# Fewer warm-up matmuls, two clamps moved to VectorE, and a residual added through the identity, with new instruction orders on all engines

## The chip, the core and the metric

The program runs on one core of one Trainium2 chip. TensorE multiplies, VectorE, ScalarE and GpSimd work on elements, and SyncE issues nearly all DMAs. The metric is the device time of one execution in microseconds; below 1% of change counts, so times stand to a hundredth.

## The reference

The input x is 2048 tokens of 448 features in bf16. A linear attention block is followed by a gated feed-forward block, each behind a layer norm and with a residual:

```python
h  = x + A_ref(layernorm(x), wqkv, wo)          # 16 heads of 28
h2 = h + B_ref(layernorm(h), w_gate, w_up, w_down)
# A: phi(t) = where(t > 0, t + 1, exp(t)) + 1e-6; pq, pk = phi(q), phi(k)
#    kv = pk^T v, z = sum(pk); o = (pq kv) / (pq z + 1e-6); o @ wo
# B: (gelu(n @ w_gate) * (n @ w_up)) @ w_down, 448 -> 1792 -> 448
```

## The kernel before, in words

The 2048 tokens are 16 tiles of 128. Every piece of work is a task with a name and an engine. Tasks know the buffers that they read and write, from which the waits on semaphores follow; in which order an engine issues its tasks is written out by hand in `ORDERS`, one string for TensorE, ScalarE, VectorE, GpSimd and SyncE each (L14 to L62). An engine takes its string strictly from left to right: a task that waits holds up everything behind it.

- **Start.** `warm1` and `warm0` (L454) are matmuls on ones whose results nobody reads; they run while the first tiles of x land. For each tile t, `bnst`/`bnag` (L462, L463) take mean and variance, `ln`/`rstd` (ScalarE) make 1/sigma, and `norm` writes xn. Tiles 0 to 3 are normalised on VectorE (L486) and transposed by TensorE (`tr`, L495), with `ev` (ScalarE, L523) copying the result to xnT. Tiles 4 to 15 are normalised on GpSimd (L487); `dup` (ScalarE, L525) repeats 64 columns, and SyncE issues one transposing DMA each (`xT4` to `xT15`, L526). SyncE has them in order of their tiles, and only behind `xT15` the loads of wo (`dwo`, four DMAs) and of the gate and up weights (`dwg`, `dwu`, 14 DMAs of 224 KB).
- **K and V.** `k`t and `v`t (L430, the helper through which most matmuls go) project a tile in pairs of 64-row matmuls, one on each half of the array. `ek` (exp, ScalarE L565), `cl` (clamp, GpSimd L566) and `ph` (VectorE L568) make phi(k); `evv` (L570) copies v; `acc`t`a`, `acc`t`b` add the tile to kv. The halves of the array change places between `a` and `b`, and a task with the other assignment waits for the earlier one. `eq`, `cq`, `pq` do for q what `ek`, `cl`, `ph` do for k. `kz1`, `kz2` (L642, L643) copy kv out with a mask.
- **Attention out.** `nd`t is pq times kv; `rd`, `om` (L654, L655) divide. Tiles 0 and 1 go by TensorE: `tro` (transpose, L681), `evo` (ScalarE), `wo` (three matmuls of 128 rows at L688, one of 64 at L689), then on VectorE `hr` (L660: PSUM plus x gives h), `hbnst`, `hbnag`, `normh`, `wrap` (L695: repeat 64 columns), and TensorE's `trh` (7 transposes, L702). From tile 2 on tiles go in pairs: `oT` (transposing DMA of o, L729, issued by SyncE behind the weight loads), `wo2a` and `wo2b` (both tiles), `hr`, the norm on GpSimd, `hT` (transposing DMA). The load of w_down, `dwd`, stands behind `oT3`.
- **Feed-forward.** `gu`n is gate and up for one slice of the 1792 columns, `ge` the gelu (ScalarE L830), `hm` the product (VectorE L832), `down` the last matmul, `out` the residual, `dout` the store. `gu` alternates between two pairs of PSUM banks, so a `gu` waits for the `hm` of the one before the last. `tbl2` loads ScalarE's table for gelu after the last exp.

Of the kernel before, what the change touches and what calls it, by code (L numbers as in the profile page):

```python
# [7 lines left out]
ALU = mybir.AluOpType  # L8
# [222 lines left out]
def bass_sequential_preLN__linear_attn_block__glu_gated_geglu__prompt_kernel(  # L231
# [5 lines left out]
    NG, GW = 4, 112  # L237
    GP = GW + 1
    NJ = FF // 128
    EPS_LN = 1e-5  # L240
    EPS = 1e-6
    HN_R = 4
    HR = 8
    O_R = 4
    QCH = 512
    NQC = S // QCH
    N_PE_TR = 4
    STAT_GROUPS = [[0], [1], [2], [3]] + [[t, t + 1] for t in range(4, T, 2)]
    EV_DVE = cfg.get("ev_dve", ())
    N_DVE_NORM = cfg.get("n_dve_norm", 4)  # L250
    N_PE_A2 = 2
    B1_CHUNKS = [2, 2, 4, 4, 4]
    WARM = 38
    WARM2 = 8
    N_END = 4
    Q_LATE = cfg.get("q_late", 5)
    SPLIT = cfg.get("split", (3, 4, 5, 6, 7))

    G = _Graph()
    es = ExitStack()  # L260
    with es:
# [45 lines left out]
        h_sb = x_sb  # L307
# [35 lines left out]
        def bank(*b):  # L343
            return [b_ps[x] for x in b]
# [568 lines left out]
```

## Time and profile before

| | us |
|---|---|
| three timed runs | 196.19, 196.21, 196.62 (median 196.21) |
| the profiled execution's own time | 196.7 |
| its span, first to last instruction | 194.9 |
| TensorE busy / VectorE / ScalarE / GpSimd | 190.3 / 116.3 / 78.2 / 42.0 |

In the profile PE is TensorE's matmuls, PEld its weight loads, DVE VectorE, ACT ScalarE, POOL GpSimd, SP SyncE; a q behind a name (SPq) is the engine's issue of a DMA. A row of the timeline gives start, length, engine, line, operation, written tile and read tiles, the shape, how many instructions are merged (x), and in brackets the engine's idle time before it with what ended it. Starts count from the first instruction of the span. Starts of single tasks named below are those of such rows.

### The profile page before, as it was taken

Reading aid. Unit: us, or ns where it says so; the run is one execution under the profiler, and the core shown is the slowest. Engines: PE = TensorE matmul, PEld = TensorE weight load, DVE = VectorE, ACT = ScalarE, POOL = GpSimd, SP = SyncE. Lnnn points to the kernel's source line nnn. Section 1 sums busy time; section 2 is a strip of 40 time slices with the busy share of each in tenths; the row PEclk is TensorE's granted clock in tenths of the full one; section 3 lists DMA queues with packets and bytes.
Section 4 is the critical chain, followed back from the end, with each engine's and each line's share of the span. In section 5 each row is a group of like instructions: output and inputs, shape, how many; then the busy total and the mean of one; then the engine's idle time right before and its main releaser. Section 6 shows DMA issues by size and latency. Waiting matters only on the chain.

```text
span 194.9 us, 5336 instructions
## 1 busy us (share of the span) xinstructions
PE 190.3 (98%) x2192; PEld 137.9 (71%) x2192; DVE 116.3 (60%) x301; ACT 78.2 (40%) x205; POOL 42.0 (22%) x90
## 2 busy tenths in 40 slices
PE   7999999999999999999999999999999999999994
PEld 7556658754588977976675577877778779899554
DVE  2989735368998946843967745756735443431512
ACT  3689866669784212220442441233232442411100
POOL 3099974300050310500500500500500000000000
PEclk9999999999999999999999999999999999999999
DMA  6944558999836052152062250172040000010111
GB/s 191 377 116 97 81 110 185 247 248 205 260 103 110 15 101 50 50 105 62 10 129 46 46 106 2 30 117 51 5 94 28 23 0 0 3 47 3 47 47 47
DMA packets 37256, 17.53 MB, mean 90 GB/s; under 512 B 28272, under 2 KB 36336, under 8 KB 37232
## 3 DMA queue, kind: packets, MB, share of 16 engines
q1 hardware_dynamic: 36352, 16.45, 36.8%
q10 hardware_dynamic: 880, 0.75, 1.2%
q8 instruction: 17, 0.28, 0.6%
q14 instruction: 7, 0.06, 0.1%
HBM read 8.72 MB, written 1.84 MB: 54 GB/s over the span
## 4 chain that ended last, share of the span: by engine, by line
PE 96%; issue 1%; ACT 1%; DVE 1%; POOL 0%; DVEq 0%; ACTq 0%; POOLq 0%
PE ps L430 87%; PE ps L780 6%; PE ps L454 2%; DVE x_sb L660 1%; PE ps L495 1%; ACT xn L617 1%; PE ps L681 0%; ACT xnT L523 0%; PE ps L672 0%; DVE x_sb L756 0%; POOL ones_bf L395 0%; POOL eps_t L398 0%; ACT pqT L616 0%; DVEq L196 0%; ACTq L196 0%
## 5 line engine op out<-in xcount | busy, mean ns | idle before, releaser
L430 PE MATMUL ps<-hnT,wgu_sb 64*128 64x512 bf16 (+1 forms) x980 | 90.4, 333 | 0.0
L430 PEld LDWEIGHTS ps<-hnT,wgu_sb 64*128 64x128 bf16 x980 | 64.5, 94 | 18.6 <-DVE hh L832 1.7
L830 ACT ACTIVATE gl<-ps 128x256 bf16<-128x256 f32 x112 | 36.9, 381 | 89.3 <-PE ps L430 88.2
L832 DVE TENSOR_TENSOR hh<-ps,gl 128x256 bf16<-128x256 f32 x112 | 42.5, 415 | 35.7 <-ACT gl L830 31.5
L430 PE MATMUL ps<-wd_sb,hh 64*128 64x448 bf16 x336 | 34.4, 349 | 0.0
L430 PEld LDWEIGHTS ps<-wd_sb,hh 64*128 64x128 bf16 x336 | 25.6, 94 | 6.2 <-DVE x_sb L756 0.2
L430 PE MATMUL ps<-wkv_sb,xnT 64*128 64x448 bf16 x192 | 22.4, 350 | 0.4 <-ACT xnT L523 0.4
L462 DVE BATCH_NORM_STATS2 st<-x_sb 128x6 f32<-128x448 bf16 x32 | 18.7, 611 | 2.6 <-DMA x_sb<-in_A_x_dram 2.6
L756 DVE TENSOR_TENSOR x_sb<-ps,x_sb 128x448 bf16<-128x448 f32 (+1 forms) x17 | 9.9, 591 | 16.6 <-PE ps L430 9.8
L474 POOL TENSOR_SCALAR ln<-mv 128x2 f32<-128x2 f32 x7 | 1.6, 223 | 75.0 <-DVE mv L463 74.9
L568 DVE SCALAR_TENSOR_TENSOR pk<-ps,tm 128x448 bf16<-128x448 f32 x16 | 9.8, 620 | 9.6 <-POOL tm L566 7.1
L430 PE MATMUL ps<-xnT,wq_sb 64*128 64x512 bf16 x112 | 14.9, 377 | 0.2 <-ACT xn L617 0.2
L430 PEld LDWEIGHTS ps<-wkv_sb,xnT 64*128 64x128 bf16 x192 | 10.1, 94 | 6.3 <-issue 0.8
L430 PE MATMUL ps<-wo_sb,oT 64*128 64x448 bf16 x98 | 12.1, 350 | 0.1
L660 DVE TENSOR_TENSOR x_sb<-ps,x_sb 128x448 bf16<-128x448 f32 x16 | 9.4, 618 | 4.6 <-PE ps L430 4.4
L780 PE MATMUL ps<-wd_sb,hh 128*128 128x448 bf16 (+1 forms) x70 | 10.8, 315 | 0.0
L566 POOL TENSOR_SCALAR tm<-e 128x448 bf16<-128x448 bf16 x16 | 8.9, 559 | 6.4 <-ACT e L565 5.5
L487 POOL TENSOR_SCALAR hn<-x_sb,nm,rs 128x448 bf16<-128x448 bf16 x14 | 10.0, 720 | 0.8 <-POOL rs L476 0.2
L565 ACT ACTIVATE e<-ps 128x448 bf16<-128x448 f32 x16 | 8.5, 541 | 3.5 <-PE ps L430 2.2
L780 PEld LDWEIGHTS ps<-wd_sb,hh 128*128 128x128 bf16 x70 | 6.7, 98 | 4.3 <-issue 0.4
L655 DVE TENSOR_TENSOR o_sb<-ps,rd 128x448 bf16<-128x448 f32 x16 | 9.4, 612 | 0.1
L570 ACT ACTIVATE v<-ps 128x448 bf16<-128x448 f32 x16 | 8.4, 542 | 2.1 <-PE ps L430 2.1
(69 smaller groups left out, 140.4 us busy)
## 6 DMA issues: line engine op xcount, KB each, us to landing
out_dram<-x_sb SPq DMA_DIRECT2D x15, 112.0 KB, 1.7
wgu_sb<-in_B_w_gate_dram SPq DMA_DIRECT2D x7, 224.0 KB, 6.1
wgu_sb<-in_B_w_up_dram SPq DMA_DIRECT2D x7, 224.0 KB, 6.4
wd_sb<-in_B_w_down_dram SPq DMA_DIRECT2D x1, 1568.0 KB, 8.3
x_sb<-in_A_x_dram SPq DMA_DIRECT2D x2, 448.0 KB, 5.3
wkv_sb<-in_A_wqkv_dram ACTq DMA_DIRECT2D x2, 336.0 KB, 3.7
x_sb<-in_A_x_dram SPq DMA_DIRECT2D x3, 224.0 KB, 4.2
wo_sb<-in_A_wo_dram SPq DMA_DIRECT2D x2, 336.0 KB, 4.4
```

What stands on the lines that cost most here:

```text
L430: ins = e.matmul(o_, l_, r_, start=s_, stop=p_, **kw)
L462: op("dve", lambda e: e.bn_stats(st[:, t, :], src_ap), [b_src], [b_st[t]], "%sbnst%d" % ("" if mv is mv1 else "h", t), 0.53, key, after=after)
L487: return lambda e: e.tensor_scalar(dst, src[:, t, :], nm[:, t:t + 1], rs[:, t:t + 1], ALU.add, ALU.mult)
L565: act_exp(lambda e: e.activation(e1[:, ie, :], oK, AF.Exp), bank(bk), [b_e1[ie]], "ek%d" % t, _c_act(D), kk)
L566: op("pool", lambda e: e.tensor_scalar(tm1[:, ie, :], e1[:, ie, :], 1.0 + EPS, 0.0, ALU.min, ALU.max), [b_e1[ie]], [b_tm1[ie]], "cl%d" % t ...
L568: op("dve", lambda e: e.scalar_tensor_tensor(pk[:, i, :, 0:GW], psK3, EPS, tm1[:, ie, :].rearrange("p (g e) -> p g e", g=NG), ALU.max, ALU ...
L655: op("dve", lambda e: e.tensor_tensor(o_sb[:, so, oc:oc + D].rearrange("p (a e) -> p a e", e=28), nd3[:, :, 0:28], rd[:, i, :].unsqueeze(2 ...
L660: op("dve", lambda e: e.tensor_tensor(h_sb[:, u, :], ps[:, b, 0:D], x_sb[:, u, :], ALU.add), bank(b) + [b_x[u]], [b_h[u]], "hr%d" % u, 0.5 ...
L756: op("dve", lambda e: e.tensor_tensor(x_sb[:, t, c0:c1], ps[:, bk, c0:c1], h_sb[:, t, c0:c1], ALU.add), bank(bk) + [b_h[t]], [bo], "out%d% ...
L780: ins = e.matmul(ps[:, bk, c0:c1], hh[:, j, hsl(t)], wd_sb[:, j, c0:c1], start=(j == 0), stop=(j == NJ - 1))
L830: G.add("act", lambda e, gi=gi, cs_=cs_, psG=psG: e.activation(gl[:, gi, cs_], psG[:, cs_], AF.Gelu_apprx_tanh), r=bank(BK_G[i]), w=[b_glh ...
L832: op("dve", lambda e, dst=dst, srcU=srcU, srcL=srcL: e.tensor_tensor(dst, srcU, srcL, ALU.mult), bank(BK_U[i]) + [b_glh], [b_ar[j_][t % HR ...
```

## The change

Four edits of code, and all five strings of `ORDERS` written anew.

```diff
+    CL_DVE = cfg.get("cl_dve", (14, 15))
-    WARM = 38
+    WARM = 33
...
-            op("pool", lambda e: e.tensor_scalar(tm1[:, ie, :], e1[:, ie, :], 1.0 + EPS, 0.0, ALU.min, ALU.max),
-               [b_e1[ie]], [b_tm1[ie]], "cl%d" % t, 0.53, kk)
+            op("dve" if t in CL_DVE else "pool", lambda e: e.tensor_scalar(tm1[:, ie, :], e1[:, ie, :], 1.0 + EPS, 0.0, ALU.min, ALU.max),
+               [b_e1[ie]], [b_tm1[ie]], "cl%d" % t, _c_dve(D, 4.0) if t in CL_DVE else 0.53, kk)
...
             def fnwo(e):
                 for g in range(3):
                     e.matmul(ps[:, bh, 0:D], oT[:, so, g, :], wo_sb[:, g, :], start=(g == 0), stop=False)
+                e.matmul(ps[:, bh, 0:D], ident[:], x_sb[:, t, :], start=False, stop=False)
                 return e.matmul(ps[:, bh, 0:D], oT[0:64, so, 3, :], wo_sb[0:64, 3, :], start=False, stop=True)
...
-            res_h(t, bh, ka)
+            op("dve", lambda e: e.tensor_copy(h_sb[:, t, :], ps[:, bh, 0:D]), bank(bh), [b_h[t]], "hr%d" % t, _c_dve(D), ka)
+            ln_stats(t, ps[:, bh, 0:D], b_ps[bh], st2, mv2, b_st2, b_mv2, ka)
...
-            def ftrh(e):
+            def ftrh(e, W):
                 ins = None
-                for k in (0, 1, 2, 4, 5, 6, 3):
+                for n, k in enumerate((0, 1, 2, 4, 5, 6, 3)):
+                    if n in (0, 6):
+                        W(n)
```

`warm0` has 33 matmuls for 38. `cl14` and `cl15` go from GpSimd to VectorE. For tiles 0 and 1, `wo` has a fifth matmul that adds x by the identity, so PSUM holds h itself: `hr` is a copy, and `hbnst` reads PSUM and no longer waits for `hr`. `trh` waits for `normh` at its first transpose and for `wrap` only at its seventh. `pkones` (VectorE's fill of pk) moves ahead of the first statistics.

The order of GpSimd in the K and V stage, of which one line reads (names between `cl4` and `cl8`):

```diff
- cl4 norm10 norm11 cl5 norm13 norm12 cl6 negm14 cq3 cq2 cl7 norm14 opad2 norm15 cl8
+ cl4 norm13 cl5 norm10 negm14 norm11 cl6 opad2 cq3 cq2 cl7 norm12 norm14 cl8 norm15
```

On GpSimd before, in the program's rows from `cl5` to `norm15` (L566 with tm<-e is a `cl`, L626 a `cq`, L487 with xn a `norm`, L481 a `negm`, L404 is `opad2`):

```order
L566 TENSOR_SCALAR tm<-e 128x448
L487 TENSOR_SCALAR xn<-x_sb,nm,rs 128x448 x2
L566 TENSOR_SCALAR tm<-e 128x448
L481 TENSOR_SCALAR nm<-mv 128x2
L626 TENSOR_SCALAR tm<-e 112x512 x2
L566 TENSOR_SCALAR tm<-e 128x448
L487 TENSOR_SCALAR xn<-x_sb,nm,rs 128x448
L404 MEMSET o_sb 128x4x64
L487 TENSOR_SCALAR xn<-x_sb,nm,rs 128x448
```

And in the change, on the same engine and stretch, from `cl5` to `norm15` (the lines count one higher):

```order
L567 TENSOR_SCALAR tm<-e 128x448
L488 TENSOR_SCALAR xn<-x_sb,nm,rs 128x448
L482 TENSOR_SCALAR nm<-mv 128x2
L488 TENSOR_SCALAR xn<-x_sb,nm,rs 128x448
L567 TENSOR_SCALAR tm<-e 128x448
L405 MEMSET o_sb 128x4x64
L627 TENSOR_SCALAR tm<-e 112x512 x2
L567 TENSOR_SCALAR tm<-e 128x448
L488 TENSOR_SCALAR xn<-x_sb,nm,rs 128x448 x2
L567 TENSOR_SCALAR tm<-e 128x448
L488 TENSOR_SCALAR xn<-x_sb,nm,rs 128x448
```

Before, the row of two norms behind `cl5` is `norm13` and `norm12`. Now `norm12` is the first of the two behind `cl7`: it moved past `cl6`, `cq3`, `cq2` and `cl7`, and `norm13` went ahead of `norm10`. ScalarE's `dup12` moved from ahead of `ek7` to behind `evv7` with it. SyncE's order of the transposes and of the loads behind them is unchanged.

On TensorE before, from the last matmuls of `qb21` to the first of the feed-forward (L688 and L689 are `wo1` and `wo0`, L430 with wo_sb are `wo2a` and `wo2b`, with wq_sb `qa31` and `qb31`, L702 `trh1` and `trh0`):

```order
L688 MATMUL ps<-wo_sb,oT 128x448 x3
L689 MATMUL ps<-wo_sb,oT 128x448
L688 MATMUL ps<-wo_sb,oT 128x448 x3
L689 MATMUL ps<-wo_sb,oT 128x448
L430 MATMUL ps<-xnT,wq_sb 128x512 x8
L430 MATMUL ps<-wo_sb,oT 128x448 x8
L430 MATMUL ps<-xnT,wq_sb 128x512 x6
L430 MATMUL ps<-wo_sb,oT 128x448 x6
L702 MATMUL ps<-ident,hn 128x128 x14
L430 MATMUL ps<-kvz,pqT 128x116 x16
```

And on TensorE in the change, the same place:

```order
L689 MATMUL ps<-wo_sb,oT 128x448 x3
L690 MATMUL ps<-x_sb,ident 128x448
L691 MATMUL ps<-wo_sb,oT 128x448
L689 MATMUL ps<-wo_sb,oT 128x448 x3
L690 MATMUL ps<-x_sb,ident 128x448
L691 MATMUL ps<-wo_sb,oT 128x448
L431 MATMUL ps<-xnT,wq_sb 128x512 x8
L431 MATMUL ps<-wo_sb,oT 128x448 x14
L707 MATMUL ps<-ident,hn 128x128 x14
L431 MATMUL ps<-xnT,wq_sb 128x512 x6
L431 MATMUL ps<-kvz,pqT 128x116 x16
```

The two identity matmuls are new, and `qb31` moved from between `wo2a` and `wo2b` to behind `trh0`.

Of the rest: TensorE has `acc13a acc14a` ahead of `qa20` and `acc15a` behind `qb20` (before: `qa20 acc13a acc14a qb20 acc14b acc15b acc15a`); ScalarE has `ek15` ahead of `evv15` and `evh0` ahead of `eq14`; VectorE has `cq10` and `cq14` behind `hm1`, and `om4`, `om5` ahead of it. Within the feed-forward some neighbouring `gu`, `ge` and `hm` change places.

More of the change, by code (lines that the diff above doesn't have):

```diff
@@ L15 @@
     "warm1 warm0 tr0 tr1 k0 v0 k1 tr2 tr3 v1 k2 acc0a k3 v2 v3 qa00 acc0b acc1b qb00 k4 acc1a acc2a v4 k5 acc2b acc3b"
[4 rows of a table removed]
[4 rows of a table added]
     " wo6b down0b nd8a gu11 nd8b gu10 gu13 gu12 down2a wo8a down2b wo8b gu15 nd10a gu14 nd10b gu17 gu16 gu19 gu18 gu21"
     " wo10a wo10b gu20 nd12a gu23 nd12b gu22 gu25 gu24 gu27 gu26 wo12a down4a wo12b gu29 nd14a gu28 nd14b gu31 down4b"
[36 rows of a table removed]
[31 rows of a table added]
+    "ones eps mhalf mones powwarm ident mask_a opad mask_b mask_c negm4 cl0 norm4 norm5 negm6 cl1 norm6 norm7 negm8"
[4 rows of a table added]
     "dx0 dx1 dx2 dwv_t dx4 dx6 dx8 dx12 dwq dwq_t dwq_u pqones xT4 xT5 xT6 xT7 xT8 xT9 xT10 xT11 xT12 xT13 xT14 xT15"
[3 rows of a table removed]
[3 rows of a table added]
 )
@@ L688, in fnwo @@
                     e.matmul(ps[:, bh, 0:D], oT[:, so, g, :], wo_sb[:, g, :], start=(g == 0), stop=False)
+                e.matmul(ps[:, bh, 0:D], ident[:], x_sb[:, t, :], start=False, stop=False)
                 return e.matmul(ps[:, bh, 0:D], oT[0:64, so, 3, :], wo_sb[0:64, 3, :], start=False, stop=True)
-            G.add("pe", fnwo, r=[b_oT[so]] + b_wo[0:2], w=bank(bh), name="wo%d" % t, dur=_c_mm(D, 4) + 0.1, key=ka, mode_end=64)
-            res_h(t, bh, ka)
+            G.add("pe", fnwo, r=[b_oT[so], b_x[t], b_ident] + b_wo[0:2], w=bank(bh), name="wo%d" % t, dur=_c_mm(D, 5) + 0.1, key=ka, mode_end=64)
+            op("dve", lambda e: e.tensor_copy(h_sb[:, t, :], ps[:, bh, 0:D]), bank(bh), [b_h[t]], "hr%d" % t, _c_dve(D), ka)
+            ln_stats(t, ps[:, bh, 0:D], b_ps[bh], st2, mv2, b_st2, b_mv2, ka)
             ln_rstd_act([t], mv2, ln2, rs2, b_mv2, b_ln2, b_rs2, ka)
@@ L703, in ftrh @@
                 return ins
-            G.add("pe", ftrh, r=[b_hn[sh], b_hnd[sh], b_ident], w=bank(bh), name="trh%d" % t, dur=_c_mm(128, 7), key=ka)
+            G.add("pe", ftrh, r=[b_hn[sh], (b_hnd[sh], 6), b_ident], w=bank(bh), name="trh%d" % t, dur=_c_mm(128, 7), key=ka, mw=True, pdt=_c_mm(128))
             hv_ = hnT[:, :, (t % HR) * 128:(t % HR + 1) * 128]
```

83 rows, old and new, of the table ORDERS are left out of this document.

## The prediction

> **What bounds the kernel now.** I read the page first, then who waits for whom, then the timeline stage by stage, then the DMAs.
>
> ```profile
> span 194.9 us, 5336 instructions
> PE 190.3 (98%) x2192; PEld 137.9 (71%) x2192; DVE 116.3 (60%) x301; ACT 78.2 (40%) x205; POOL 42.0 (22%) x90
> ```
>
> TensorE is busy for 98% of the span, VectorE for 60%. Of TensorE's waits (us in total, times, longest) the two long ones are these:
>
> ```profile
> PE ps L430 <- POOL mhalf L401: 1.0, 1, 1.0
> PE ps L430 <- ACT xnT L523: 0.4, 1, 0.4
> ```
>
> So the end moves by what the change takes from or adds to TensorE's queue: matmuls, and waits. The first wait is for the ones of the warm-up, the second for tile 0, and two of 0.2 us stand in brackets in the rows at 49.21 and 53.47 below. Behind 54 us the feed-forward is one dense block. The question is which waits are there afterwards.
>
> **The start.**
>
> ```profile
> 1.93 4.24 PE L454 MATMUL ps<-ones_bf 128*128 128x128 bf16 x38
> ...
> 5.21 0.37 DVE L486 TENSOR_SCALAR xn<-x_sb,mv,rs 128x448 bf16<-128x448 bf16 x1
> ...
> 5.97 0.40 DVE L486 TENSOR_SCALAR xn<-x_sb,mv,rs 128x448 bf16<-128x448 bf16 x1
> ...
> 6.10 0.96 PE L495 MATMUL ps<-ident,xn 64*128 64x64 bf16 x20
> ...
> 7.43 0.74 PE L430 MATMUL ps<-wkv_sb,xnT 64*128 64x448 bf16 x6 [0.36 <-ACT xnT L523]
> ```
>
> The 38 warm-up matmuls take 4.24 us, 0.11 each; `norm0` is done at 5.58, yet `tr0` starts at 6.10, behind the last of them. Five fewer end 0.55 us earlier, at which point `tr0` waits for `norm0`: about 5.63, so 0.46 us is gained. `tr1` then waits for `norm1` (6.37, little earlier by moving `pkones`), but `k0` needs only tile 0: it goes from 7.43 to 6.97. Bounds: 0 (if `k0` is held by something unseen) and 0.55.
>
> **K and V.** In the chain of work that ended last, one piece reaches from 10.5 to 37.5 us, 336 matmuls without a wait, so the 0.46 us are kept.
>
> ```profile
> 10.51 27.04 PE ps L430 x336
> ```
>
> With `cl14` and `cl15` on VectorE, GpSimd's clamp (0.56) and a hand-over go:
>
> ```profile
> 37.27 0.56 POOL L566 TENSOR_SCALAR tm<-e 128x448 bf16<-128x448 bf16 x1 [1.78 <-ACT e L565]
> ...
> 37.96 0.62 DVE L568 SCALAR_TENSOR_TENSOR pk<-ps,tm 128x448 bf16<-128x448 f32 x1 [1.71 <-POOL tm L566]
> ```
>
> A clamp on VectorE is bounded by its norm of the same shape, 0.37, and by GpSimd's 0.56; I take 0.37. `ph14` ends at about 38.2 instead of 38.58, but the new order wants it for `acc14a` at 38.15, ahead of `qa20` instead of behind it, and `evv15`, which frees a bank for `qa20`, now runs behind `ek15`. The order takes what the clamp gives: 0, between 0.2 gained and 0.3 lost.
>
> **The residual of tiles 0 and 1.**
>
> ```profile
> 47.02 0.74 PE L688 MATMUL ps<-wo_sb,oT 128*128 128x448 bf16 x3
> ...
> 48.05 1.93 ACT L617 ACTIVATE xn<-ps 112x1024 bf16<-112x1024 f32 x2
> 48.10 0.62 DVE L660 TENSOR_TENSOR x_sb<-ps,x_sb 128x448 bf16<-128x448 f32 x1
> ...
> 49.21 1.04 PE L430 MATMUL ps<-xnT,wq_sb 64*128 64x512 bf16 x8 [0.19 <-ACT xn L617]
> ...
> 50.07 0.94 PE L430 MATMUL ps<-wo_sb,oT 64*128 64x448 bf16 x8
> ...
> 52.16 0.95 PE L702 MATMUL ps<-ident,hn 128*128 128x128 bf16 x14
> ...
> 53.47 0.82 PE L430 MATMUL ps<-kvz,pqT 49*128 49x116 bf16 x15 [0.21 <-DVE x_sb L660]
> ...
> 54.13 7.89 PE L430 MATMUL ps<-hnT,wgu_sb 64*128 64x256 bf16 x140
> ```
>
> Two identity matmuls of 448 columns are 2 x 0.19 (three take 0.74, which overlap). Of that, 0.19 lies in the wait that `qa31` has anyway for ScalarE, so +0.2. VectorE's chain to `trh` loses the step from `hr` to `hbnst`. I take 0.62 for a `hbnst` that reads PSUM and for the copy, as for the addition at L660, which reads the same bank; 0.5 and 0.7 would move nothing below, since VectorE is no longer the last to be waited for. From `wo2a` to `gu1` it is 4.06 us now. In the new order: `wo2a` 0.75 (its 0.94 less the overlapping end of the last), a change of halves between `wo2a` and `wo2b` 0.23 (an estimate from the 0.17 to 0.19 by which a matmul's end outlasts its turn, and the signal), `wo2b` 0.57 (six of such eight), a switch and 14 transposes 0.95, `qb31` 0.65 (six of the eight that start at 49.21 and give way at 50.07), `nd4a`, change, `nd4b` 0.65: 3.8. So -0.25, since `qb31` fills the wait for `hr3`. `tbl2` now stands behind `evh0` and `eq14`, so the first gelu is some 0.4 us later and `gu3` may wait for `hm1`: +0.1 (0 to 0.4).
>
> Without more, that is -0.46 + 0.2 - 0.25 + 0.1, or 0.4 us gained. But `wo2a` also needs `oT2` and `oT3`, which come by DMA.
>
> **The queue behind norm12.** GpSimd and ScalarE around tile 12, and SyncE's issues:
>
> ```profile
> 20.72 1.41 POOL L487 TENSOR_SCALAR xn<-x_sb,nm,rs 128x448 bf16<-128x448 bf16 x2
> ...
> 24.55 0.71 POOL L487 TENSOR_SCALAR xn<-x_sb,nm,rs 128x448 bf16<-128x448 bf16 x1
> ```
> ```profile
> 23.38 0.54 ACT L565 ACTIVATE e<-ps 128x448 bf16<-128x448 f32 x1
> ```
> ```profile
> L526 SPq DMA_TRANSPOSE xnT<-xn x1: 1189/1189/1189, 23.5 to 23.5; - x1
> ```
> ```profile
> 11.65 16.94 SPq L526 DMA_TRANSPOSE xnT<-xn  x12
> 28.64 3.19 SPq L364 DMA_DIRECT2D wo_sb<-in_A_wo_dram  x4
> ...
> 40.91 0.60 SPq L364 DMA_DIRECT2D wgu_sb<-in_B_w_up_dram  x1
> 45.48 2.51 SPq L729 DMA_TRANSPOSE oT<-o_sb  x2
> ```
>
> `norm12` ends at 22.13 and its transpose is issued at 23.5. In the change `norm12` stands behind `cl7`, which needs `ek7` (23.38, tied to TensorE; `cl7` ends where `norm14` starts), so it takes the place that `norm14` has now, 24.55, less about 0.3 for TensorE's lead. It ends near 25.0, `dup12` (0.26) near 25.3, and `xT12` is issued there: **1.8 us later**. `xT12` to `xT15` are issued one right behind the other, 1.19 to 1.31 us each, so nothing is made up, and wo and the 14 weight loads start 1.8 us later. Bounds for this delay: 1.6 (lead of 0.46) to 2.1 (none).
>
> Do `oT2` and `oT3` then come later? Issue to landing, last column, for the last weight load and the two transposes, and the DMA share by stage (second to last number):
>
> ```profile
> wgu_sb<-in_B_w_up_dram SPq DMA_DIRECT2D x1, 224.0 KB, 7.5
> ```
> ```profile
> oT<-o_sb SPq DMA_TRANSPOSE x1, 3.5
> ```
> ```profile
> oT<-o_sb SPq DMA_TRANSPOSE x1, 2.6
> ```
> ```profile
> 30.00:34.00 4.00, 4.00 (x50) 3.26 (x46) 2.03 (x4) 2.62 (x6) 2.16 (x4) 1.00 0.78 214
> 34.00:44.00 10.00, 9.87 (x140) 6.28 (x135) 5.04 (x12) 6.16 (x11) 1.82 (x4) 1.00 1.01 249
> 44.00:47.00 3.00, 3.00 (x36) 1.26 (x33) 2.43 (x7) 2.80 (x4) 0.00 (x0) 1.00 1.00 236
> ```
> ```profile
> DMA to landing us min/median/max: 2.4/2.5/4.2
> ```
>
> The engines of the DMA are full from 34 to 47 us. The last weight load lands at 40.9 + 7.5 = 48.4, and `oT2`, issued at 45.5, only at 49.0, 3.5 us later, where the median of the 14 such transposes is 2.5 (last row); `oT3`, issued at 46.7, lands at 49.3. They come right behind the weights, which I read as one queue, served in order. Now the margin to `wo2a` (50.07) is 0.7. With weights 1.8 us later, `oT3` lands at about 51.15, while TensorE would be there at 50.07 - 0.46 + 0.2 = 49.8. It **waits 1.4 us**, and all that was gained earlier is lost in that wait. Behind `wo2a` on TensorE stand `wo2b`, `trh1`, `trh0`, `qb31` and `gu1`; ScalarE's `evh0` and first gelu, and VectorE's `hr2` and `hr3`, wait for these, so nothing of the feed-forward can start meanwhile.
>
> The Trainium skill, "DMA: Bandwidth & Descriptors", section "Queues, rings and completion order", says that descriptors are consumed in ring order on each engine, but that completion is not first in, first out for an issuing engine. By its first half the transposes wait as above; the second half leaves room for one that lands early. No row here shows one overtaking.
>
> **The sum.** Against the profiled execution, 196.7: `wo2a` goes from 50.07 to 51.15 plus 0.05 for the signal, +1.13; -0.25 up to `gu1`; +0.1 at `gu3`: +1.0, so **197.7**, with one term behind `gu1` still to be costed, the next pair's transposes:
>
> ```profile
> wd_sb<-in_B_w_down_dram SPq DMA_DIRECT2D x1, 1568.0 KB, 8.3
> ```
> ```profile
> 56.29 3.53 SPq L729 DMA_TRANSPOSE oT<-o_sb  x2
> ...
> 61.77 0.54 PE L430 MATMUL ps<-wo_sb,oT 64*128 64x448 bf16 x3
> ```
>
> w_down, which lands at 48.0 + 8.3 = 56.3, is 1.8 us later too, and `oT4` and `oT5` behind it. The first is issued at 56.3 and takes at most 4.2 (the longest of the row above), so it lands by 60.5, and the second soon after, ahead of `wo4a` at 61.77, which itself starts 0.9 later: I take 0, at most 0.4.
>
> The timed median, 196.21, is 0.5 below the profiled run, with one of three at 196.62; I keep the profiled base, so the measured difference may be 1.0 to 1.5. About 0.3%, 0.6 us, is what can be told from no change.
>
> **Rivals.**
>
> *Not slower: the transposes are not held by the weights.* If `oT2` takes 2.5 us from its issue (45.0), it lands at 47.5, no wait arises, and the gains stand: 196.7 - 0.4 = 196.3, or 195.8 if the base is the median. It decides when `oT3` lands before 49.8. For it: the median of 2.5. Against it: the 3.5 us, and landings 0.3 to 0.6 apart right behind 48.4. I give 0.11.
>
> *Half the delay.* The DMA share from 30 to 34 is 0.78, so 0.9 us of transfer fit there; if a later start packs the loads closer, the delay is 0.9, `oT3` lands at 50.3, and the sum is +0.1: 196.8. Against it: the gaps come from SyncE's issue, which moves as one. 0.08.
>
> *The clock comes late.*
>
> ```profile
> 11.88 0.73 PE L430 MATMUL ps<-wkv_sb,xnT 64*128 64x448 bf16 x6
> ```
>
> Rows of the start show TensorE slow and then fast: a warm-up matmul of 128 columns takes 0.11; from 7.43 six k matmuls, three pairs of 448 columns, take 0.74, as 0.73 at 11.88, which is twice that rate. By 7.43, then, the rate had doubled, after 5 us of warm-up. With less warm-up and a gap ahead of `tr1` it may double some 3 us later; the 1.5 us or more of k and v work in that stretch would take twice as long, which moves `ek7` and all behind it: 197.7 + 1.5 = 199.2. For it: less dense work ahead. Against it: the gaps are only 0.2 to 0.5 us. 0.07.
>
> The Trainium skill, "TensorE: Matmul & The Clock Gate", Part 1, speaks against this edit: the clock doubles after a busy window of about 3.4 us that runs free of the kernel's start. By it, a run whose window falls early has faster warm-ups and gains less from dropping five, and one whose window is missed pays the stretch above. No row here shows the phase of other runs.
>
> **How the numbers follow.** Forecast 0.74, 197.7, own range 197.0 to 198.6 (delay 1.6 to 2.1, `gu3` and `wo4a` up to 0.7 worse, the base up to 0.5 lower). Slower by over 0.6 us holds in it, in the late clock and in half of the half delay: 0.85. The first rival is mostly within 0.6 us: 0.11 the same, 0.04 faster. The range of 8 in 10 reaches from 196.6 to 198.9 and leaves out the first rival and the late clock.
>
> **What would show it.** `tr0` near 5.6 and `k0` near 7.0 for the start; `xT12` issued near 25.3, wo near 30.4; the last weight load landing near 50.2; `oT3` near 51.1; a wait of TensorE of 1 to 2 us ahead of the wo_sb matmuls at L431, where there was none; `gu1` near 55.0 instead of 54.13, and a feed-forward of the same length. A landing of `oT3` below 50 with late weights would make the prediction wrong.

## The result and the profile after

Before: 196.31 us, median of 12 executions (196.17 to 196.74). Changed: **197.64 us**, median of 12 (196.46 to 200.42). The ratio of the two, which leaves the two highest executions (199.66 and 200.42) out as disturbed, is 1.005, with an interval of 1.003 to 1.0071: slower. The profiled execution of the change took 197.88, and its span is 1.2 us longer than that of before. The page begins:

```profile
span 196.1 us, 5331 instructions
...
PE 190.4 (97%) x2189; PEld 127.3 (65%) x2189; DVE 116.9 (60%) x303; ACT 77.8 (40%) x205; POOL 42.0 (21%) x88
```

TensorE works as long as before (190.4 us against 190.3). What the span gained in length is wait. The start of the timeline, TensorE's rows:

```profile
1.93 3.54 PE L455 MATMUL ps<-ones_bf 128*128 128x128 bf16 x33
5.79 0.41 PE L496 MATMUL ps<-ident,xn 64*128 64x64 bf16 x10 [0.31 <-DVE xn L487]
6.57 0.41 PE L496 MATMUL ps<-ident,xn 64*128 64x64 bf16 x10 [0.37 <-DVE xn L487]
6.99 0.74 PE L431 MATMUL ps<-wkv_sb,xnT 64*128 64x448 bf16 x6
```

The bracketed waits show `tr0` and `tr1` waiting for `norm0` and `norm1`; `k0` starts at 6.99, 0.44 earlier. Then GpSimd and SyncE at tile 12 (the second row is the answer for the single transpose `xT12`, issued at 25.4):

```profile
24.41 1.42 POOL L488 TENSOR_SCALAR xn<-x_sb,nm,rs 128x448 bf16<-128x448 bf16 x2
```
```profile
L527 SPq DMA_TRANSPOSE xnT<-xn x1: 1190/1190/1190, 25.4 to 25.4; - x1
```

`norm12` begins at 24.41 instead of 21.42, behind `cl7`, and the transpose goes out 1.9 us later. The loads and the transposes of o behind it, first SyncE's issues (start, length), then from issue to landing (last column) for the last weight load, `oT2` and `oT3`:

```profile
30.86 2.63 SPq L365 DMA_DIRECT2D wo_sb<-in_A_wo_dram  x4
...
41.74 0.60 SPq L365 DMA_DIRECT2D wgu_sb<-in_B_w_up_dram  x1
44.90 2.51 SPq L734 DMA_TRANSPOSE oT<-o_sb  x2
```
```profile
wgu_sb<-in_B_w_up_dram SPq DMA_DIRECT2D x1, 224.0 KB, 8.1
```
```profile
oT<-o_sb SPq DMA_TRANSPOSE x1, 5.4
```
```profile
oT<-o_sb SPq DMA_TRANSPOSE x1, 4.7
```

The last weight lands at 41.74 + 8.1 = 49.8 (48.45 before). `oT2`, issued 0.6 earlier than before, takes 5.4 us and lands at 50.3; `oT3`, issued at 46.15, lands at 50.8 (49.4 before). TensorE there:

```profile
48.64 1.05 PE L431 MATMUL ps<-xnT,wq_sb 64*128 64x512 bf16 x8
50.38 0.35 PE L431 MATMUL ps<-wo_sb,oT 64*128 64x448 bf16 x1 [0.70 <-DVE hn L487]
50.94 1.71 PE L431 MATMUL ps<-wo_sb,oT 64*128 64x448 bf16 x13 [0.21 <-DMA oT<-o_sb]
52.59 0.96 PE L707 MATMUL ps<-ident,hn 128*128 128x128 bf16 x14
...
54.79 0.93 PE L431 MATMUL ps<-hnT,wgu_sb 64*128 64x256 bf16 x14
```

Two waits stand ahead of `wo2a`'s first two matmuls, which in the kernel make one pair, one on each half of the array: the first reads `oT2`, the second `oT3`. The first wait is put down to VectorE's hn, which `wo2a` doesn't read; what it reads is `oT2`, landed at 50.3. The second names the DMA itself. In the chain of work that ended last, `oT3` is now a piece, which it wasn't before:

```profile
46.15 4.66 DMA oT<-o_sb
50.80 0.14 issue
50.94 0.93 PE ps L431 x7
```

`gu1` starts at 54.79, 0.66 later than before. From there to the end of the span it is 141.3 us, where it was 140.8. These 0.5 us are the second loss, in the feed-forward, which the prediction had at 0.1.

### The profile page after: what moved, and what is told of

It reads as the page before. It is cut to its first block, busy times and chain, and to the rows that moved or that the text cites. A ratio compares the mean times of both kernels' runs of the same rounds, so it can differ in the third digit from the quotient of the medians.

```text
span 196.1 us, 5331 instructions
## 1 busy us (share of the span) xinstructions
PE 190.4 (97%) x2189; PEld 127.3 (65%) x2189; DVE 116.9 (60%) x303; ACT 77.8 (40%) x205; POOL 42.0 (21%) x88
## 4 chain that ended last, share of the span: by engine, by line
PE 88%; DMA 4%; DVE 4%; ACT 2%; issue 1%; SPq 0%; DVEq 0%
PE ps L431 81%; PE ps L785 5%; DMA oT<-o_sb 2%; DMA x_sb<-in_A_x_dram 2%; DVE hh L837 1%; ACT L855 1%; DVE pqT L620 1%; PE ps L496 1%; ACT hnT L712 0%; ACT pqT L617 0%; PE ps L707 0%; DVE pqT L619 0%; DVE o_sb L656 0%; DVE st L463 0%; PE ps L673 0%
## 5 line engine op out<-in xcount | busy, mean ns | idle before, releaser
L431 PE MATMUL ps<-hnT,wgu_sb 64*128 64x512 bf16 (+1 forms) x980 | 91.8, 333 | 0.1
L431 PEld LDWEIGHTS ps<-hnT,wgu_sb 64*128 64x128 bf16 x980 | 61.4, 94 | 23.4 <-DVE hh L837 4.9
L431 PE MATMUL ps<-wd_sb,hh 64*128 64x448 bf16 x336 | 35.3, 349 | 0.0
L431 PEld LDWEIGHTS ps<-wd_sb,hh 64*128 64x128 bf16 x336 | 20.8, 94 | 11.6 <-DVE x_sb L761 0.2
L463 DVE BATCH_NORM_STATS2 st<-x_sb 128x6 f32<-128x448 bf16 x30 | 17.4, 612 | 2.5 <-DMA x_sb<-in_A_x_dram 2.5
L482 POOL TENSOR_SCALAR nm<-mv 128x2 f32<-128x2 f32 x13 | 3.0, 230 | 60.4 <-DVE mv L464 60.1
L431 PE MATMUL ps<-wo_sb,oT 64*128 64x448 bf16 x98 | 13.0, 350 | 1.1 <-DVE hn L487 0.7
L661 DVE TENSOR_TENSOR x_sb<-ps,x_sb 128x448 bf16<-128x448 f32 x14 | 8.2, 618 | 6.0 <-PE ps L431 6.0
L566 ACT ACTIVATE e<-ps 128x448 bf16<-128x448 f32 x16 | 8.7, 542 | 3.7 <-PE ps L431 2.2
L431 PEld LDWEIGHTS ps<-wo_sb,oT 64*128 64x128 bf16 x98 | 6.3, 94 | 5.2 <-PE ps L431 1.5
L567 POOL TENSOR_SCALAR tm<-e 128x448 bf16<-128x448 bf16 x14 | 7.9, 564 | 4.2 <-ACT e L566 3.7
```

What stands on the lines that cost most here:

```text
L431: ins = e.matmul(o_, l_, r_, start=s_, stop=p_, **kw)
L463: op("dve", lambda e: e.bn_stats(st[:, t, :], src_ap), [b_src], [b_st[t]], "%sbnst%d" % ("" if mv is mv1 else "h", t), 0.53, key, after=after)
L566: act_exp(lambda e: e.activation(e1[:, ie, :], oK, AF.Exp), bank(bk), [b_e1[ie]], "ek%d" % t, _c_act(D), kk)
L567: op("dve" if t in CL_DVE else "pool", lambda e: e.tensor_scalar(tm1[:, ie, :], e1[:, ie, :], 1.0 + EPS, 0.0, ALU.min, ALU.max), [b_e1[ie] ...
L661: op("dve", lambda e: e.tensor_tensor(h_sb[:, u, :], ps[:, b, 0:D], x_sb[:, u, :], ALU.add), bank(b) + [b_x[u]], [b_h[u]], "hr%d" % u, 0.5 ...
```

## The experiments

Each kernel was timed beside the kernel before on the same chip. "Late" below means an execution that lies 1.3 us or more above the median of the others of its kernel, and "common" are those others; the first experiment shows what a late one is.

**1. norm12 early again** (the change, with tile 12 to 15's order as before):

```diff
- norm11 cl6 opad2 cq3 cq2 cl7 norm12 norm14 cl8 norm15
+ norm11 norm12 cl6 opad2 cq3 cq2 cl7 norm14 norm15 cl8
```

> The changed kernel with one thing put back: GpSimd's norm12 ahead of cl6 and norm15 ahead of cl8, and ScalarE's dup12, dup14 and dup15 ahead of the copies that they stood behind, as before. Theory of the queue (norm12 late, so xT12, wo and the weights late, so oT3 lands late): xT12 is issued near 23.3 instead of 25.4, the last weight load lands near 48.2 instead of 49.8, oT3 near 49.2 instead of 50.8, no wait of TensorE of 0.2 us or more ahead of wo2a, gu1 near 53.5 (54.79 in the change, 54.13 before), and the time falls by 1.0 to 1.4 us below the change, to 196.3 to 196.7. Rival, the wait belongs to TensorE's own chain (wo1, wo0 with the fifth matmul, qa31, ScalarE's copy) and the landing only looks like its end: gu1 stays at 54.5 to 54.8 and the time within 0.3 of the change. If the spread of the changed kernel's times (196.5 to 200.4) comes from the landing that TensorE now waits for, the five times lie within 0.6 us; if it comes from the start or from the feed-forward, they spread as in the change.

Median 196.81; nine of 12 lie from 196.56 to 196.93, three at 198.2 to 198.5. Ratio to before 1.0027 (1.0002 to 1.0053). The wait is gone; TensorE's rows at `qa31` and `wo2a`:

```profile
50.49 1.05 PE L431 MATMUL ps<-xnT,wq_sb 64*128 64x512 bf16 x8
51.38 1.75 PE L431 MATMUL ps<-wo_sb,oT 64*128 64x448 bf16 x14
```

No bracket, and 3.88 us from `wo2a` to `gu1` (55.26). But the time stays 0.19 above the kernel before (nine executions, median 196.70, against 196.51), where the prediction had counted on 0.4 below it without this wait. And the profiled execution was one of the three late ones: by `qa31` (50.49) it is 1.85 us behind the change, and the loss lies at the start. So the landings and the `gu1` that were expected above can't be compared with it.

```profile
1.93 3.70 PE L455 MATMUL ps<-ones_bf 128*128 128x128 bf16 x33
...
7.30 1.30 PE L431 MATMUL ps<-wkv_sb,xnT 64*128 64x448 bf16 x6
...
9.03 1.88 PE L431 MATMUL ps<-wkv_sb,xnT 64*128 64x448 bf16 x12
```

Six matmuls of k take 1.30 where they took 0.74, twelve take 1.88 where they took 1.31: TensorE goes at half its rate until 10.2, where single matmuls of 448 columns fall from 0.58 us to 0.35. This is the prediction's third rival, the clock that comes late, met in a kernel with 33 warm-ups. `oT3` lands at 51.28 here, 0.1 ahead of `wo2a`, so by this trace alone the wait could also have been swallowed by TensorE's lateness; experiment 6 settles that.

**2. norm12 late alone** (the kernel before, only `norm12` behind `cl7` and `dup12` behind `evv7`):

```diff
- norm13 norm12 cl6 negm14 cq3 cq2 cl7 norm14
+ norm13 cl6 negm14 cq3 cq2 cl7 norm12 norm14
```

> The kernel before with one thing of the change alone: norm12 behind cl7 on GpSimd (ahead of norm14), dup12 behind evv7 on ScalarE, nothing else. Theory of the queue: xT12 is issued near 25.7 (23.5 before), wo and the weights follow 1.8 to 2.2 later, oT3 lands near 51.3 (49.3 before), TensorE waits 1.0 to 1.4 us ahead of wo2a, gu1 starts near 55.3 (54.13 before), and the time is 1.0 to 1.5 us above the kernel before: 197.3 to 197.8. Rival, the slack in SyncE's queue takes up the delay, or the weights pack closer: oT3 by 50.0 and the time within 0.4 of the kernel before. The spread grows beyond 1 us if the wait for the landing makes it, and stays within 0.6 otherwise.

Median 197.88, ratio 1.0059 (1.003 to 1.0087): as large as the whole change. `oT3` lands at 51.37 and `gu1` starts 1.42 later. But the wait makes only part of it. TensorE's rows at `qa10` and `wo2a`:

```profile
27.60 0.38 PE L430 MATMUL ps<-xnT,wq_sb 64*128 64x512 bf16 x1
28.25 1.02 PE L430 MATMUL ps<-xnT,wq_sb 64*128 64x512 bf16 x7 [0.28 <-ACT e L565]
...
51.05 1.37 PE L430 MATMUL ps<-wo_sb,oT 64*128 64x448 bf16 x8 [0.31 <-DVE st L462]
```

A norm put behind `cl7` pushes `norm15` and `cl8` as well; `ph8` comes at 27.48 instead of 26.95, and `qa10`'s second matmul waits for a bank; what follows `qa10` starts 0.46 late (28.92 against 28.46). About 0.5 is lost there, 0.5 ahead of `wo2a`, and 0.4 behind its first matmul, where the second waits for `oT3` (the eight take 1.37 instead of 0.94). So the landing makes some 0.9 of the 1.42, and a late `norm12` is enough to make a kernel this slow, but not by the queue alone, as I had expected.

**3 and 4. The warm-ups alone**: the change with `WARM = 38`, and the kernel before with `WARM = 33`.

> The changed kernel with 38 warm-up matmuls again, all else as in the change. By my theory the 0.44 us that the start gained are lost in the wait ahead of wo2a anyway, since GpSimd's norm12 waits for cl7, which follows TensorE by less than one for one: k0 near 7.4, the wait ahead of wo2a shorter by 0.1 to 0.4, the time 0.0 to 0.4 above the change. Rival, the late clock: with 33 warm-ups the rate of TensorE doubles late in some executions, and this makes the change's median and its spread; then with 38 the times lie within 0.6 us of each other and the median is 0.5 or more below the change.

> The kernel before with 33 warm-up matmuls, nothing else. By the sum the start gains 0.44 (tr0 near 5.7, k0 near 7.0), nothing behind it waits for it, since oT3 had a margin of 0.7 us and cl7 moves norm12 by nothing: gu1 near 53.7 and the time 0.3 to 0.45 below the kernel before. Rival, the late clock: the median is not below that of the kernel before, or single times lie 1 us or more above the others.

The change with 38: median 198.23 (six executions), ratio 1.0091 (1.0056 to 1.0127). Its interval overlaps that of the change, so that it is slower than with 33 isn't clear of the noise; in its trace `gu1` starts at 55.12, 0.33 later than with 33. By this trace 0.33 of the 0.44 at `k0` reach `gu1` through the wait, since the whole stage, GpSimd's clamps with it, moves with `k0`. The kernel before with 33: `k0` at 7.08 and `gu1` at 53.79, 0.35 and 0.34 earlier, and nothing lost up to the end. Seven of the 12 executions lie from 196.12 to 196.65 (median 196.34), but five at 198.0 or above, so that the ratio is 1.0019 (0.9989 to 1.0048). The gain of the start is small, 0.34 in the trace and 0.17 between the common times (196.34 against 196.51); the late executions that come with it take it away.

**5. The transposes ahead of two weight loads** (the change, SyncE's order):

```diff
- dwg6 dwu6 oT2 oT3 dwd
+ oT2 oT3 dwg6 dwu6 dwd
```

(The code of `oT` also drops an argument that only bound `oT2` and `oT3` into the order behind the loads.)

> The changed kernel with SyncE's issues of oT2 and oT3 moved ahead of the last two weight loads (dwg6, dwu6), all else as in the change, norm12 late included. If the landing of oT3 is what TensorE waits for and DMAs of one queue are served in order, two loads of 224 KB fewer stand ahead of it: at 0.55 to 0.6 us between landings of weights, oT3 lands 0.8 to 1.2 us earlier, near 49.7 instead of 50.8, the wait ahead of wo2a shrinks to 0.0 to 0.3, gu1 starts near 53.8 to 54.1 and the time falls 0.7 to 1.0 below the change; the displaced loads still land by 53. Rival, the DMA engines are shared among all transfers in flight, so the order within the queue does not matter: oT3 within 0.3 us of 50.8 and the time within 0.3 of the change. Another rival: the feed-forward needs all fourteen loads, and dwu6, issued behind oT3, lands later than gu1 wants it (54): then gu1 waits for the weights instead and nothing is gained.

Nine of 12 from 196.46 to 197.39, median of all 196.79, ratio 1.0022 (1.0003 to 1.0041). So most of the loss goes though `norm12` stands as late as in the change. Its profile is again a late execution, of another kind, so its landings say little:

```profile
PEclk9789999999999999999999999999999999999999
```
```profile
1.93 3.13 PE L455 MATMUL ps<-ones_bf 128*128 128x128 bf16 x33
6.10 0.41 PE L496 MATMUL ps<-ident,xn 64*128 64x64 bf16 x10 [1.04 <-DVE xn L487]
...
8.69 2.42 PE L431 MATMUL ps<-wkv_sb,xnT 64*128 64x448 bf16 x12
```

TensorE's granted clock there is the third number from the end:

```profile
4.40:7.60 3.20, 1.78 (x36) 1.24 (x35) 2.25 (x6) 1.59 (x6) 0.00 (x0) 1.00 1.10 369
7.80:11.00 3.20, 3.14 (x20) 0.99 (x17) 3.15 (x11) 1.95 (x8) 0.62 (x2) 0.50 1.11 375
11.20:14.00 2.80, 2.80 (x48) 1.68 (x46) 2.06 (x7) 2.42 (x9) 2.21 (x6) 1.00 0.03 6
```

The 33 warm-ups are done in 3.13 us, the last ten at twice the rate, from 4.3 on. Then TensorE waits 1.04 us for `norm0`, and from 7.7 to 11.1 it is back at half the rate: the row of the clock, one digit for 5 us, falls to 7 and 8.

**6. The parts that the runs left standing** (run last): the change's K and V stage with its late `norm12`, its identity matmuls and PSUM reads, the two loads behind `oT3` as in 5, from `nd0` on the orders of before, 36 warm-ups.

> A kernel put together from what the runs have shown: of the change the K and V stage as it is (clamps of tiles 14 and 15 on VectorE, norm12 late), the identity matmuls and the reads of PSUM; SyncE with oT2 and oT3 ahead of the last two weight loads; from nd0 on the orders of all engines as before (qb31 between wo2a and wo2b, eq14 ahead of evh0); 36 warm-ups. Theory: TensorE's lead at nd0 is 0.3 to 0.5 (0.2 from the start, 0.15 to 0.3 from the K and V stage), oT3 lands by 49.8, the wait ahead of wo2a is 0.0 to 0.3, nothing is lost at gu3, gu5 or nd6a, and the common time is 196.0 to 196.35, 0.2 to 0.5 below the kernel before. Rival, the last weights, issued behind oT3, land later than gu1 wants them, or oT3 still lands at 50.5: the time is that of the kernel before or 0.3 above it.

`xT12` is issued at 25.6, later than in the change, and still, from issue to landing of `oT2` and `oT3` and on TensorE:

```profile
oT<-o_sb SPq DMA_TRANSPOSE x1, 3.0
```
```profile
oT<-o_sb SPq DMA_TRANSPOSE x1, 2.5
```
```profile
48.78 1.05 PE L431 MATMUL ps<-xnT,wq_sb 64*128 64x512 bf16 x8
49.65 0.93 PE L431 MATMUL ps<-wo_sb,oT 64*128 64x448 bf16 x8
```

With 448 KB fewer ahead of it in the queue, `oT3` (issued at 46.30) lands at 48.8 instead of 50.8, and TensorE goes on without a wait, at its normal clock. It differs from the change in more than the queue, but `qa31` starts within 0.14 of the change's (48.64), so TensorE is ready for `wo2a` at the same point and now finds `oT3` there. This shows the queue: a late `norm12` costs nothing at `wo2a` once two of the loads between are gone. `gu1` starts at 53.74, 0.39 earlier than before. Of that 0.17 is left at the end of TensorE's work; steps of 0.02 to 0.08 in the feed-forward take the rest, whose cause stays open. The time is 196.57 against 196.45, ratio 1.0008 (0.9999 to 1.0018): no gain, where 0.2 to 0.5 had been expected.

**7 and 8. hm3 first** (experiment 1, and on VectorE the following; then the same with `WARM = 38`):

```diff
- hm1_0 hm1_1 cq14 cq10 hm0_1 hm0_0 wrap3 pq10 wrap2 hm3_1 hm3_0 pq12
+ hm1_0 hm1_1 cq14 hm0_1 hm0_0 wrap3 hm3_1 hm3_0 cq10 wrap2 pq10 pq12
```

> The kernel with norm12 early again (33 warm-ups), and on VectorE hm3 moved ahead of cq10, wrap2 and pq10, so that gu5 does not wait for hm3. In the trace of the change gu5's second pair starts 0.29 late, because hm3 stands behind wrap2, which stands behind GpSimd's normh2. Theory: the 0.3 us at gu5 go, wo4a comes 0.3 earlier against gu1 than in the change, nothing later gives it back: 196.2 to 196.4 in the executions whose clock is early, 0.3 below the same kernel without this edit (196.66) and 0.1 to 0.3 below the kernel before. Rival: the wait is only moved, to hm2 or to hT2 behind the later wrap2: the time within 0.1 of 196.66. About one execution in four lies 1.6 to 2 us above the others, if 33 warm-ups are what makes the clock late.

> The same kernel as the one with hm3 first, with 38 warm-up matmuls. Late clock theory: of 12 executions at most one lies 1.6 us or more above the others (with 33 warm-ups three or four), and the common ones are 0.2 to 0.4 above those with 33: 196.5 to 196.7. Rival, the late executions have nothing to do with the count of warm-ups: as many of them as with 33. Ahead of wo2a no wait of 0.2 us or more; k0 at 7.43.

Ratios 1.0044 (1.0024 to 1.0064) and 1.0025 (1.0016 to 1.0034): worse than expected. The rival was right that the wait only moves, though neither to where it said nor within its 0.1: the common executions with 33 have their median at 196.96. This is the feed-forward's loss. The rows before, of VectorE, GpSimd and ScalarE:

```profile
58.92 0.68 DVE L619 TENSOR_TENSOR pqT<-xn,pqT 112x1024 bf16<-112x1024 bf16 x1
59.52 0.75 DVE L832 TENSOR_TENSOR hh<-ps,gl 128x256 bf16<-128x256 f32 x2
```
```profile
57.11 1.41 POOL L487 TENSOR_SCALAR hn<-x_sb,nm,rs 128x448 bf16<-128x448 bf16 x2
```
```profile
54.08 1.28 ACT L850 ACT_TABLE_LOAD   x1
```

In the change, VectorE's, GpSimd's, ScalarE's and TensorE's rows at the first gelus:

```profile
57.88 0.78 DVE L619 TENSOR_SCALAR pqT<-pqT 112x1024 bf16<-112x1024 bf16 x2
...
59.43 1.04 DVE L620 TENSOR_TENSOR pqT<-xn,pqT 112x1024 bf16<-112x1024 bf16 x1
60.39 0.26 DVE L754 COPY hn<-hn 128x448 bf16<-128x448 bf16 x1
60.58 0.74 DVE L837 TENSOR_TENSOR hh<-ps,gl 128x256 bf16<-128x256 f32 x2
```
```profile
57.88 2.06 POOL L488 TENSOR_SCALAR hn<-x_sb,nm,rs 128x448 bf16<-128x448 bf16 x2
```
```profile
54.39 1.02 ACT L617 ACTIVATE pqT<-ps 112x1024 bf16<-112x1024 f32 x1
55.43 1.28 ACT L855 ACT_TABLE_LOAD   x1
```
```profile
62.81 0.54 PE L431 MATMUL ps<-wo_sb,oT 64*128 64x448 bf16 x3
```

And in its chain of work that ended last, `hm3` and then TensorE from `gu5`'s second matmul on:

```profile
60.66 0.68 DVE hh L837 x2
...
61.38 2.47 PE ps L431 x35
```

`qb31` behind `trh0` makes `eq14` late (54.39), the table of gelu later by 1.35 (it was loaded by 55.36, now by 56.71), and puts `cq14`, `cq10` and `pq10` between `hm1` and `hm3`. `hm3` starts at 60.58, 5.79 behind `gu1`, where it was 5.39, and `gu5` waits 0.3 for it: from `gu1` to `wo4a` it is 8.02 instead of 7.64. Put first, `hm3` no longer holds `gu5`, but what stood ahead of it now stands ahead of `hr5`, and `nd6a` waits for that (the kernel with 38 warm-ups):

```profile
64.76 0.21 PE L431 MATMUL ps<-kvz,pqT 64*128 64x116 bf16 x1
65.14 0.38 PE L431 MATMUL ps<-kvz,pqT 49*128 49x116 bf16 x7 [0.17 <-DVE x_sb L661]
```

So the 0.3 of `gu5` are gone, but from `gu1` to the end of TensorE's work it is 139.0 us, where it is 138.9 in the change and 138.3 before. Of late executions, the kernel with 33 had four of 12, the same with 38 none of 12.

**9 and 10. The residual's part alone** on the kernel before (the code of the diff for `wo`, `hr`, `hbnst`, `trh`). First with `qb31` behind `trh0`, `evh0` ahead of `eq14`, and `cq10`, `cq14` behind `evh1`; then with only `hbnst` ahead of `hr` on VectorE and every other order as before:

> The kernel before with the residual's part of the change alone: the identity matmul in wo0 and wo1, hr as a copy with hbnst reading PSUM ahead of it, trh with its two waits, TensorE's order wo2a wo2b trh1 trh0 qb31, evh0 ahead of eq14. No change of warm-ups, clamps or norm12. By the sum: wo0 starts 0.2 later, qa31 at the same time as before, wo2a within 0.1 of 50.07, from wo2a to gu1 3.8 to 3.95 instead of 4.06, gu3 or gu2 0.07 later from the late first gelu: gu1 near 54.0 and the time 0.0 to 0.2 below the kernel before. Rival: the two identity matmuls cost their 0.38 in full and the reordering returns nothing: gu1 near 54.4 and the time 0.2 to 0.4 above the kernel before.

> The kernel before with the identity matmuls, hr as a copy, hbnst reading PSUM ahead of hr, and trh with two waits, but with all orders of TensorE, ScalarE, GpSimd and SyncE as before (qb31 between wo2a and wo2b, eq14 ahead of evh0, cq14 behind evh1). Theory: the 0.7 us that the residual's part cost in the earlier run come from qb31 behind trh0, which makes eq14, the load of gelu's table and cq14 late, so that hm1 is late for gu3 (0.63 of wait there), not from the two matmuls or from reading PSUM. Then gu1 starts at 54.1 to 54.25 (54.13 before), gu3's second pair waits for nothing, and the time is 0.0 to 0.15 above the kernel before: 196.4 to 196.65. Rival, the two matmuls of 448 columns and the reads of PSUM cost on the path themselves: gu1 near 54.4 or a wait at gu3 of 0.3 or more, and the time 0.3 to 0.7 above the kernel before.

The first: ratio 1.0034 (1.0023 to 1.0045), 197.22 against 196.51. `gu1` starts 0.15 earlier than before, yet `gu3`'s second matmul waits:

```profile
57.77 2.47 PE L430 MATMUL ps<-hnT,wgu_sb 64*128 64x256 bf16 x42 [0.47 <-DVE hh L836]
```

(where I had put `cq14`, ahead of `hbnst2`, it makes `hm1` still later than the change does, so 0.7 is the price of this order and not of the change's). The second: ratio 1.0003 (0.9994 to 1.0012). The two matmuls and the reads of PSUM cost nothing and bring nothing; only the orders that were written with them cost.

**11 and 12. What makes the clock late.** The kernel before with 33 warm-ups and short matmuls on ones in the gaps behind them; and with 36 warm-ups:

```diff
- warm1 warm0 tr0 tr1 k0
+ warm1 warm0 tr0 warm2 tr1 warm3 k0
```

> The kernel before with 33 warm-up matmuls, and with ten short matmuls on ones put into TensorE's two gaps behind them: three pairs of 116 columns between tr0 and tr1, two pairs between tr1 and k0. Nothing waits for them, and the gaps (0.5 and 0.3 us in the trace with 33 warm-ups) hold their 0.3 and 0.2. Theory: the rate of TensorE changes at fixed distances of some 3.4 us and is high only behind a stretch in which TensorE was busy nearly throughout; with 33 warm-ups the gaps ahead of tr0, tr1 and k0 fall into that stretch, and in a third of the executions (14 of 47, where 38 had 2 of 78) k and v run 3 us at half the rate. Then with the gaps filled at most one of 12 executions lies 1.5 us or more above the others, k0 starts at 7.0 to 7.15, and the common time is that of 33 warm-ups without late ones, 196.1 to 196.45, with a median 0.1 to 0.35 below the kernel before. Rival, only the length of the unbroken warm-up counts: three or four of 12 executions lie at 198 or above, as with 33 warm-ups alone, and the median is that of the kernel before.

> The kernel before with 36 warm-up matmuls, nothing else. In the traces so far a warm-up at the low rate takes 0.107, so 36 end 0.21 before 38 do: tr0 near 5.9, k0 near 7.2, and 0.2 gained in the executions with an early clock (196.2 to 196.4 in common). Theory: the share of executions in which k and v run 3 us at half the rate grows as the unbroken warm-up gets shorter (38: 2 of 78; 33: 14 of 47; filling the gaps behind 33 did not lower it, 3 of 12), so that 36 has one or two of 12. Rival: the share steps, and 36 has as few as 38 (0 of 12) or as many as 33 (3 to 5 of 12).

Filling did not help: three of 12 late, ratio 1.0019 (0.9997 to 1.004); my theory of the gaps, as far as these ten matmuls fill them (0.5 us ahead of `tr0` stay), fell. With 36 none of 11 is late, but the 0.15 by which the trace is earlier can't be seen in the time: ratio 1.0001 (0.9992 to 1.001). The trace of before is of an execution of 196.7, some 0.2 above the medians of that kernel here, so a gain read against it looks that much too large. Counted over all kernels in which no spread of a landing hides it: 38 warm-ups 2 late of 146, 36 none of 22, 33 alone 15 of 48 (the expectations counted 2 of 78 and 14 of 47). No kernel that was run beats the one before by what can be measured.

## Why the prediction was right, point by point

- **The start** was to give 0.46 at `k0`; it gave 0.44 in the profiled execution, which is the large end: over the traces `k0` starts between 6.99 and 7.31 with 33 warm-ups and between 7.21 and 7.43 with 38. What was underrated is the late clock: a chance of 0.07 for a price of 1.5, where about three of ten executions with 33 warm-ups pay 1.4 to 1.9 (one 3.1). The profiled execution of the change, 197.88, has no late clock and lies above the median, so the median needs no late ones.
- **K and V** at 0, within 0.2 gained: `nd0` is 0.58 early, so 0.14 more than the start.
- **The identity matmuls** were to cost 0.2, the other 0.2 lying in `qa31`'s wait. They cost nothing: `wo1` starts 0.58 early, `wo0` 0.39, `qa31` 0.57 again, and experiment 10 agrees. So TensorE could have begun `wo2a` at 48.64 + 0.87 = 49.51 (the spacing is that of experiment 6, 48.78 to 49.65), where 49.8 was said.
- **The queue behind norm12**, on which the forecast rested: `xT12` at 25.4 (25.3 said), the last weight at 49.8 (50.2), `oT3` at 50.8 (51.1). Experiment 6 shows the cause. But the delay wasn't kept one for one, as the prediction had argued when it gave "half the delay" 0.08: the first load of wo is issued 2.2 later than before, the last weight load only 0.8 (41.74 against 40.91), and it lands 1.35 later. The queue made up a part.
- **The wait** was said to be 1.4, and it is: from 49.51 to `gu1` at 54.79 are 5.28, and 3.88 without the wait (experiment 1). That the number agrees is partly luck, since the wait began and ended some 0.3 earlier than said, each for a reason of its own (the two points above).
- **From wo2a to gu1**, 3.8 said: 3.88 without the wait (experiment 1).
- **The mis-sized term** is the one behind `gu1`: +0.1 for `gu3` and 0 for `wo4a`. `gu3` was 0.07, but `wo4a` came 0.38 late against `gu1`, not by `oT4` (landed at 58.75, four us ahead) but by VectorE's queue at `hm3`, and 0.16 more was lost later. Nor was w_down 1.8 late: issued at 47.45 and 7.7 on its way, it landed at 55.1, ahead of the 56.3 of before. "A feed-forward of the same length" was wrong.
- **The sum** was +1.0 and measured 1.2 between the profiled executions: `gu1` was 0.2 less late than said (54.79, not 55.0) and the feed-forward 0.4 longer. That these two nearly cancel is luck. So is that 197.7 meets the median of 197.64: it counts from the profiled 196.7, which lies 0.4 above the median before (196.31); from median to median the loss is 1.33.
- The **first rival's price**, 195.8 to 196.3, was too low, for the larger part by the same term: with the wait removed the kernel stands at 196.70 in its common executions.

The spread of the changed kernel's times (196.46 to 198.31 without the two highest) is wider than that of a kernel without a wait for a landing (196.56 to 196.93 in the common executions of experiment 1). That the landing's own variation makes it is argued, not shown: the other executions have no trace.

## What to carry to other kernels

A step that is moved on one engine moves every DMA queued behind it; look for the last consumer of that queue, not for the next one, and ask which bulk loads stand ahead of a small transfer that the busy engine needs. How much of the delay arrives there is read from the landings: here 1.9 us at the start of the queue were 1.4 at its end. A wait taken from a busy neighbour shows up as the next one in its queue, so a reordering is worth only what is left at the end of the stage. An earlier start that rests on fewer warm-ups is to be judged by all executions, not by the best or by one profile.

## What the runs showed of the hardware

- TensorE's rate stepped at distances of 3.4 us: in experiment 5 up at 4.3, down at 7.7, up at 11.1; in experiment 1 it stepped up only at 10.2. The same 33 warm-ups took 3.13, 3.54 or 3.70 us. The row of the clock shows the step down (7, 8) but not the late step up of experiment 1, where every slice reads 9; the durations of equal matmuls show both. The Trainium skill, "TensorE: Matmul & The Clock Gate", Part 1, says that the clock follows a window of about 3.4 us that runs free of the kernel's start, and the distances in experiment 5 agree. That both kinds of late clock come from the idle time between the warm-ups and `k0` fits these traces (1.04 and 0.38 us of it lie between the steps at 4.3 and 7.7) but isn't shown: experiment 11 filled a part of that time, and as large a share of its executions was late.
- One queue was served in order: `oT2` landed 0.5 to 0.6 behind the last load issued ahead of it, whether it had itself been issued 3.0 us earlier (experiment 6), 3.5 (before) or 5.4 (the change).
- GpSimd and VectorE slowed each other: the pair of norms at 57.88 took 2.06 us where it took 1.41 before, while VectorE ran `cq14`, `cq10` and `pq10`, and `pq10` took 1.04, where a product of the same shape took 0.68 before. The Trainium skill, "SBUF — State Buffer", section "Who interferes with whom", has the two share a pair of ports of which one blocks the other; these rows agree that they collide.
